# Performer attention and gated feed-forward on one core: squares moved to GpSimd, five more lean key chunks, small products in tiles of the array, and a new order

## The chip, the cores and the metric

The kernel runs on one core of one Trainium2 chip. The metric is the device time of one execution in microseconds, as the median of several runs. The engines are TensorE (PE; its weight loads are listed apart as PEld), VectorE (DVE), ScalarE (ACT), GpSimd (POOL) and SyncE (SP, which issues nearly all transfers). Each engine takes its instructions strictly in the order in which they were issued to it.

## What is computed

```python
def _attn_ref(q, k, v, omega):                 # 8 batches, 8 heads, 576 tokens, 64 wide; 128 features
    scale = 1.0 / np.sqrt(np.sqrt(D))
    q_s, k_s = (q * scale, k * scale)
    def phi(x):
        proj = np.einsum('bhsd,md->bhsm', x, omega)
        sq = np.sum(x * x, axis=-1, keepdims=True) / 2.0
        h = proj - sq
        h = h - np.max(h, axis=-1, keepdims=True)
        return np.exp(h) / np.sqrt(m)
    q_p, k_p = (phi(q_s), phi(k_s))
    kv = np.einsum('bhsm,bhsd->bhmd', k_p, v)
    z = np.sum(k_p, axis=2)
    num = np.einsum('bhsm,bhmd->bhsd', q_p, kv)
    den = np.einsum('bhsm,bhm->bhs', q_p, z)[..., None] + 1e-06
    return num / den

def _moe_ref(x, w_gate, w_val, w_out, rms_g):  # x: 4608 x 512; hidden width 1536
    xn = x / np.sqrt(np.mean(x * x, axis=-1, keepdims=True) + 1e-06) * rms_g
    g = xn @ w_gate
    return (g * (1.0 / (1.0 + np.exp(-g))) * (xn @ w_val)) @ w_out
```

q, k, v and omega are fp32. The three weight matrices come as fp64 and are turned into fp32 on the chip (`weights`, lines 414 to 484).

## The kernel before

The 4608 tokens are 36 chunks of 128. A pair of batches fills nine chunks, so that the middle one (number 4 of the nine) holds 64 tokens of either batch.

**Features** (`features`, for `k` and `q`, 36 chunks each). SyncE loads the chunk: for a plain chunk 512 KB, the transposed input for the projection beside the natural one for the norm; for a *lean* chunk (the first four of `k` and of `q`) the transposed 256 KB alone. `square` squares the input on ScalarE (with a factor of 1/4 ahead of the square, so 1/16 in the result). A plain chunk sums the squares per head with a VectorE reduction (`norm`, line 653); a lean chunk does it on TensorE, with the squares as stationary operand against a constant `heads2` (`norm_pe`, line 617: four products of 128 rows by 128 columns, 96 columns moving). `project` (line 666) multiplies by omega with the array split into two halves of 64 rows; `peak` takes the maximum per head on VectorE (line 679), `shift` forms the bias (lines 684 and 687), and `exps` writes the features with eight ScalarE exponentials (line 696). The first `k` chunk adds its bias by a product (`move`) instead.

**Keys times values.** `kv_half` accumulates the four whole chunks of a batch in halves of 64 array columns (line 797). `kv_mid` handles the shared middle chunk, four times in all: per head one product of 128 rows by 128 columns against a value tile of 130 columns, in which each batch's half stands beside zeros (loaded from `vmid`, 520 KB), three heads to a PSUM bank, with six evictions on VectorE (lines 758 and 768).

**Attention and normalisation** (`attend`): transposes of the query features (line 830), the product with `kv` in halves of 64 columns (line 841), the division on VectorE, the sum of squares on ScalarE, the root and the low part of the split on GpSimd (lines 873, 876, 910), and transposes back (line 891).

**Feed-forward.** The first three of twelve hidden slices run as three-pass products (`gated`, tile `ff`, line 303 and the two after it) as soon as a block of tokens is there. At about 380 us the remaining nine slices begin with a seven-product scheme (`unit`), at about 769 us the output with a fifteen-product one (`out_triple`). The change doesn't touch these.

**Order.** `Plan` writes the order of every engine by hand. Each step is added with an engine, a cost, a key of urgency, what it follows, and the slots it takes and gives; a list scheduler then hands the free engine its ready step of the lowest key. On TensorE, feed-forward steps (keys of 900 and more) come behind all others, and among the others a step in the array's present form (`rows`, `columns`, `full`) goes first; a change of form is charged 0.17. As long as no feed-forward step is ready, an idle TensorE is given a dummy product, `spin` (line 1036). The keys stand in the table `KEYS`; those of a chunk are the sum of a few entries, with fixed small offsets for each kind of step (as `key - 0.3`).

```python
        s = add("ACT", 0.54, square, [i], key)
        sq = ("psM", "sq", nm)
        if not lean:
            s = add("DVE", 0.62, norm, [s], key)
        p = add(
            "PE", 0.9, project, [i], key, [("psJ", nm, 0), ("psJ", nm, 1), (tag + "p", c)],
            mode="rows",
        )
        if lean:
            s = add("PE", 0.9, norm_pe, [s, p] if not first else [s], key, [sq])
```

Of the kernel before, what the change touches and what calls it, by code (L numbers as in the profile page):

```python
# [18 lines left out]
M = 128  # L19
DM = H * D  # L20
DFF = 1536
P = 128
# [20 lines left out]
    "lead": 2.76,  # L43
    "v": 94.42,
    "kv": -1042.79,
    "ks": [-482.1, 29.96, -132.79, -264.03, -121.88, -50.15, -91.33, -322.02, -18.14, -22.8, -48.17, -24.72, -44.53, -44.85, -5.61, -5.94, -12.97, -3.84, 2.1, 1.55, 8.44, 5.02, 7.82, 13.18, 14.51, 8.53, 67.56, 437.89, 70.53, 124.42, 9.96, 167.4, 229.45, 437.17, 436.87, 679.48],
    "qs": [-339.21, 60.83, -85.07, -28.07, -51.09, -68.82, -41.84, -8.68, -33.39, -36.86, -11.44, -13.61, -12.77, 3.74, 0.93, 9.58, 2.88, 13.96, 13.82, 24.74, 16.19, 27.63, 23.68, 32.28, 44.1, 39.37, 46.63, 71.79, 74.09, 51.71, 125.65, 141.98, 159.63, 160.11, 205.61, 233.21],
    "turns": [-103.42, 24.18, -177.68, -590.21, -266.4, -604.12, 86.86, -213.13, -649.06, -162.44, -441.45, -1049.27, 220.46, -465.51, -315.47, -515.05, 120.4, -151.51, -498.12, 49.51, 140.45, 37.25, -640.45, -581.4, -246.73, -220.97, -81.01, -127.83, 485.02, 422.3, 324.99, 129.53, 519.61, -510.45, -277.71, 106.54],
    "mixes": [-148.66, 18.01, -233.73, -283.22, -460.75, -241.78, -153.65, -610.2, -526.4, -237.05, -205.9, -687.04, -21.23, -169.25, -42.57, -535.29, -651.31, -129.56, -8.22, -36.89, -110.15, 62.57, 73.55, 66.58, -366.23, -288.34, 215.05, 358.84, -231.21, 414.57, -331.48, -648.64, 347.15, 23.97, 508.45, 389.85],
    "kvs": [65.82, -394.35, 257.28, -625.61, 216.21, -194.21, -511.95, 647.67],  # L50
    "attend": -122.15,
# [6 lines left out]
LEAN = {"k": 4, "q": 4}  # L58
# [10 lines left out]
        "ink": (4, 1), "v": (6, 1), "vm": (1, 1), "kp": (7, 1), "inq": (3, 1), "qp": (2, 1),  # L69
# [78 lines left out]
WIDE = 96  # L148
# [160 lines left out]
def performer_glu_kernel(  # L309
# [5 lines left out]
    vmid: bass.AP,  # L315
# [72 lines left out]
    for i in range(2):  # L388
        nc.gpsimd.memset(heads2[i * D : (i + 1) * D, 0, i : i + 1], 1.0 / SCALE)
        nc.gpsimd.memset(heads2[i * D : (i + 1) * D, 1, i : i + 1], 1.0)  # L390
# [199 lines left out]

    def features(tag, c, key):
# [5 lines left out]
        lean = c < max(LEAN[tag], FIRST[tag])  # L597

# [10 lines left out]
        def square():  # L609
            n = t["raw"][:, 1, :]  # L610
            nc.scalar.activation(n, t["x"] if lean else n, AF.Square, scale=0.25)

        def norm_pe():
            sq = tile_("psM", [P, DM], f"sq{nm}")
            t["sq"] = sq[:, :H]
            for hp in range(4):
                nc.tensor.matmul(
                    sq[:, 2 * hp : 2 * hp + WIDE],
                    lhsT=t["raw"][:, 1, hp * P : (hp + 1) * P],
                    rhs=heads2[:, 0 if first else 1, :],  # L620
                    start=True,
                    stop=True,
                    skip_group_check=True,
                )
# [26 lines left out]
        def norm():  # L651
            t["sq"] = small("sq", f"sq{nm}")
            ve.tensor_reduce(
                out=t["sq"],
                in_=t["raw"][:, 1, :].rearrange("p (h d) -> p h d", d=D),
                axis=AX.X,
                op=ALU.add,
            )
# [45 lines left out]
        size = 0.26 if lean else 0.52  # L704
# [11 lines left out]
        add("NONE", 0, lambda: None, [s, p], key, give=[("in" + tag, c)])  # L716
        m0 = add("DVE", 0.62, lambda: peak(0), [p], key)
        m1 = add("DVE", 0.62, lambda: peak(1), [m0], key)
        if first:
            b = add("DVE", 0.3, shift_first, [m1, s], key, give=[sq])  # L720
# [9 lines left out]
        b = add("DVE", 0.3, shift, [m1, s], key, give=[sq] if lean else [])  # L730
        e = b
        for n in range(4):
            e = add("ACT", 0.51, lambda n=n: exps(n), [e], key - 0.3, give=[("psJ", nm, n // 2)] if n % 2 else [])
        st["exp", tag, c] = e

    def values(c, key):
        mid = c % 9 == 4
        tag = "vm" if mid else "v"

        def load():  # L740
            w = 2 * (D + 1) if mid else D + 1
            st["v", c] = tile_(tag, [P, H, w], f"v{c}")
            nc.sync.dma_start(st["v", c], vmid[c // 9] if mid else va[c])

        size = 0.53 if mid else 0.27
        st["vload", c] = add("SP", size / RATE, load, key=key, take=[(tag, c)], land=LAND)

    def kv_mid(pr, key):
# [3 lines left out]
        def heads(h0, n, t):  # L752
            if h0 == 0:
                for b in range(2):
                    st["kv", 2 * pr + b] = tile_("kv", [P, H, D + 1], f"kv{2 * pr + b}")
            t["pt"] = tile_("psM", [P, 3, 2 * (D + 1)], f"kvm{pr}_{h0}")
            for i in range(n):
                nc.tensor.matmul(
                    t["pt"][:, i, :],
                    lhsT=st["kp", c][:, h0 + i, :],  # L760
                    rhs=st["v", c][:, h0 + i, :],
                    start=True,
                    stop=True,
                )

        def out(h0, n, t):
            for b in range(2):
                ve.tensor_scalar_mul(
                    st["kv", 2 * pr + b][:, h0 : h0 + n, :],
                    t["pt"][:, :n, b * (D + 1) : (b + 1) * (D + 1)],  # L770
                    1.0 / M,
                )

        last = [st["exp", "k", c], st["vload", c]]
        for h0 in (0, 3, 6):
            n = min(3, H - h0)
            t = {}
            ps = ("psM", "kvm", pr, h0)
            take = [ps] + ([("kv", 2 * pr), ("kv", 2 * pr + 1)] if h0 == 0 else [])
            give = [("kp", c), ("vm", c)] if h0 == 6 else []  # L780
            m = add("PE", 0.24 * n, lambda a=(h0, n, t): heads(*a), last, key, take, give)
            last = [m]
            done.append(add("DVE", 0.29, lambda a=(h0, n, t): out(*a), [m], key, give=[ps]))
# [36 lines left out]
    def attend(c, ahead, key):  # L820
# [100 lines left out]
        for half in range(2):  # L921
# [4 lines left out]
            te.append(add("ACT", 0.5, lambda h=half: turned(h), [i], ahead - 0.4,  # L926
# [896 lines left out]
```

## Time and profile before

| | |
|---|---|
| time, median of 3 runs | 1021.58 us (1021.27 to 1021.89) |
| span of the profiled execution, first to last instruction | 1020.1 us |
| busy share of the span: PE, PEld | 99%, 84% |
| busy share: DVE, ACT, POOL | 84%, 65%, 18% |
| granted clock of TensorE | full in every slice |
| transferred | 213.93 MB, mean 210 GB/s |

Of the profiled execution only the span is given; it is 1.5 us under the median of the runs, which also hold what lies around the program. TensorE's busy time includes the dummy products, and records of products overlap, so that a pace is read from starts, not from lengths. Each fp32 product appears as two records.

### The profile page before, as it was taken

Reading aid. Unit: us, or ns where it says so; the run is one execution under the profiler, and the core shown is the slowest. Engines: PE = TensorE matmul, PEld = TensorE weight load, DVE = VectorE, ACT = ScalarE, POOL = GpSimd, SP = SyncE. Lnnn points to the kernel's source line nnn. Section 1 sums busy time; section 2 is a strip of 40 time slices with the busy share of each in tenths; the row PEclk is TensorE's granted clock in tenths of the full one; section 3 lists DMA queues with packets and bytes.
Section 4 is the critical chain, followed back from the end, with each engine's and each line's share of the span. In section 5 each row is a group of like instructions: output and inputs, shape, how many; then the busy total and the mean of one; then the engine's idle time right before and its main releaser. Section 6 shows DMA issues by size and latency. Waiting matters only on the chain.

```text
span 1020.1 us, 20747 instructions
## 1 busy us (share of the span) xinstructions
PE 1007.7 (99%) x7628; PEld 857.4 (84%) x7628; DVE 857.2 (84%) x1505; ACT 666.8 (65%) x1477; POOL 179.4 (18%) x259
## 2 busy tenths in 40 slices
PE   9999999999999999999999999999999999999998
PEld 6889888888888888888898888988888887888886
DVE  6899899998976765998889958988778999789885
ACT  7999999898796646646356446643556554565561
POOL 0323212221223338100001123000000000222120
PEclk9999999999999999999999999999999999999999
DMA  9677676585544476674576767775456684898882
GB/s 315 233 243 236 221 250 228 186 275 166 193 146 146 139 234 214 205 258 145 170 251 213 238 203 243 241 259 196 151 179 235 226 292 152 202 273 191 204 175 63
DMA packets 120805, 213.93 MB, mean 210 GB/s; under 512 B 10496, under 2 KB 53248, under 8 KB 120704
## 3 DMA queue, kind: packets, MB, share of 16 engines
q1 hardware_dynamic: 115808, 203.69, 60.1%
q0 software_dynamic: 4896, 8.92, 6.1%
q8 instruction: 60, 0.98, 0.4%
q14 instruction: 41, 0.34, 0.1%
HBM read 134.58 MB, written 77.99 MB: 208 GB/s over the span
## 4 chain that ended last, share of the span: by engine, by line
PE 83%; DVE 9%; ACT 6%; issue 1%; DMA 0%; SPq 0%; ACTq 0%; DVEq 0%
PE q L304 8%; PE q L305 8%; PE q L303 8%; PE pa L303 7%; PE pa L304 7%; PE pa L305 7%; PE ff L303 4%; PE ff L305 4%; PE ff L304 4%; PE pb L304 4%; PE pb L305 4%; PE pb L303 4%; PE nu L841 2%; PE pc L304 2%; PE pc L305 2%; PE pc L303 2%
## 5 line engine op out<-in xcount | busy, mean ns | idle before, releaser
L1290 ACT ACTIVATE c<-c 128x512 f32<-128x512 f32 (+1 forms) x90 | 52.9, 590 | 90.2 <-DVE c L1272 90.0
L303 PE MATMUL ff<-xhi,whi 128*128 128x512 f32 (+3 forms) x248 | 94.6, 381 | 1.5 <-ACT qp L696 0.6
L1686 POOL DMA_DIRECT2D out_dram<-c x34 | 29.8, 885 | 360.6 <-ACT c L1672 290.6
L696 ACT ACTIVATE qp<-pjq,biq 128x128 f32<-128x128 f32 x288 | 81.1, 431 | 15.0 <-DVE biq L687 12.5
L305 PE MATMUL ff<-xhi,wlo 128*128 128x512 f32 (+3 forms) x248 | 90.4, 365 | 0.0
L304 PE MATMUL ff<-xlo,whi 128*128 128x512 f32 (+3 forms) x248 | 90.3, 364 | 0.0
L696 ACT ACTIVATE kp<-pjk,bik 128x128 f32<-128x128 f32 x280 | 78.7, 447 | 5.7 <-DVE bik L687 2.8
L910 POOL TENSOR_TENSOR xlo<-xr,xhi 128x256 fp32r<-128x256 f32 x72 | 56.3, 807 | 125.2 <-ACT xhi L907 125.2
L1554 DVE TENSOR_TENSOR hb<-hb,hb 128x1024 f32<-128x1024 f32 x55 | 66.3, 1219 | 0.4
L303 PEld LDWEIGHTS ff<-xhi,whi 128*128 128x128 f32 x248 | 46.7, 188 | 10.3 <-ACT qp L696 0.8
L305 PEld LDWEIGHTS ff<-xhi,wlo 128*128 128x128 f32 x248 | 46.7, 188 | 7.6
L304 PEld LDWEIGHTS ff<-xlo,whi 128*128 128x128 f32 x248 | 46.8, 189 | 6.2
L1272 DVE TENSOR_TENSOR c<-pb,u 128x512 f32<-128x512 f32 (+1 forms) x45 | 28.4, 633 | 27.3 <-PE pb L305 25.2
L679 DVE TENSOR_REDUCE mxk<-pjk 128x4 f32<-128x512 f32 x72 | 46.9, 682 | 4.7 <-PE pjk L666 4.7
L1265 ACT COPY m<-pa 128x512 f32<-128x512 f32 (+1 forms) x45 | 24.4, 543 | 34.9 <-PE pa L305 34.7
L679 DVE TENSOR_REDUCE mxq<-pjq 128x4 f32<-128x512 f32 x72 | 46.5, 681 | 0.8 <-PE pjq L666 0.8
L833 ACT COPY qpT<-qt 128x512 f32<-128x512 f32 x72 | 41.1, 664 | 1.9 <-PE qt L830 1.9
L841 PEld LDWEIGHTS nu<-kv,qpT 128*64 128x64 f32 x1152 | 36.0, 137 | 5.3 <-issue 1.1
L830 PE MATMUL qt<-ident,qp 128*128 128x128 f32 x288 | 38.6, 276 | 1.6 <-DVE hmk L684 1.0
L666 PE MATMUL pjq<-front,inq 64*128 64x128 f32 x560 | 39.8, 281 | 0.1
L841 PE MATMUL nu<-kv,qpT 128*64 128x65 f32 x1152 | 39.6, 223 | 0.1
L1109 POOL TENSOR_TENSOR lw_0l<-wr,lw_0h 128x256 fp32r<-128x256 f32 x9 | 7.7, 854 | 182.0 <-PE pa L305 138.5
(300 smaller groups left out, 3254.0 us busy)
## 6 DMA issues: line engine op xcount, KB each, us to landing
hb<-h_scratch SPq DMA_DIRECT2D x49, 512.0 KB, 5.4
h_scratch<-c SPq DMA_DIRECT2D x72, 256.0 KB, 2.5
ink<-in_kx_dram SPq DMA_DIRECT2D x32, 512.0 KB, 5.2
inq<-in_qx_dram SPq DMA_DIRECT2D x32, 512.0 KB, 4.5
Xb<-xn_scratch SPq DMA_DIRECT2D x28, 512.0 KB, 5.2
f<-in_wgv_dram SPq DMA_DIRECT2D x24, 512.0 KB, 4.9
xn_scratch<-xr SPq DMA_DIRECT2D x36, 256.0 KB, 3.2
out_dram<-c SPq DMA_DIRECT2D x36, 256.0 KB, 2.9
```

The lines of the kernel that those rows point to most:

```text
L303: nc.tensor.matmul(out, lhsT=ah, rhs=bh, start=first, stop=False, skip_group_check=again)
L304: nc.tensor.matmul(out, lhsT=ah, rhs=bl, start=False, stop=False, skip_group_check=again)
L305: nc.tensor.matmul(out, lhsT=al, rhs=bh, start=False, stop=last, skip_group_check=again)
L666: nc.tensor.matmul(t["pts"][i][:, hp, :], lhsT=x[rows, hp, :], rhs=om[rows, :], start=hp == 0 or not first, stop=True, skip_group_check=first,
L679: ve.tensor_reduce(out=by_half[:, i, :], in_=t["pts"][i], axis=AX.X, op=ALU.max)
L696: nc.scalar.activation(st[tag + "p", c][:, h, :], t["pts"][h % 2][:, h // 2, :], AF.Exp, bias=t["bi"][:, h : h + 1], scale=SCALE,)
L830: nc.tensor.transpose(t["pt", half][:, i, :], st["qp", c][:, 4 * half + i, :], ident)
L833: nc.scalar.copy(t["qpT"][:, 4 * half : 4 * half + 4, :], t["pt", half])
L841: nc.tensor.matmul(pt[lo:hi, i, :], lhsT=t["qpT"][:, h, lo:hi], rhs=st["kv", b][:, h, :], start=True, stop=True,)
L910: nc.gpsimd.tensor_tensor(out=st["xT", blk][1][:, ccs, cs], in0=t["xr"][:, ccs], in1=st["xT", blk][0][:, ccs, cs].bitcast(F32), op=ALU.sub ...
L1290: nc.scalar.activation(t[nm], t[nm], AF.Silu)
L1554: ve.tensor_tensor(out=t[nm, g], in0=t[x, g], in1=t[y, g], op=ALU.add if sign == "+" else ALU.subtract,)
```

## The change

- `LEAN` for `k` goes from 4 to 9 chunks: chunks 4 to 8 of `k` load 256 KB instead of 512 KB, and their norm goes from VectorE to TensorE.
- `square` runs on GpSimd for the first 14 chunks of `k` and of `q` (28 squares), without the factor. Lean chunks take the factor 1/16 in `heads2`; plain ones among the 28 (ten of `q`, five of `k`) get a step `quarter` on GpSimd behind the reduction.
- `norm_pe` becomes eight products on halves of 64 array columns, with 64 columns moving (`WIDE` from 96 to 64).
- `kv_mid` becomes, per head, four products on quarters of the array (64 rows by 64 columns, 65 moving): the two batches lie on different rows and go to PSUM tiles of their own. Half of the heads at a time take two banks; there are four evictions instead of six. The tile `vm` and the input `vmid` go; the middle chunk loads 260 KB like any other, and the value pool grows from six to seven.
- The features of `q` chunk 0, whose load also brings omega, are added first, and every projection follows that load in the plan.
- All keys are replaced. Sixteen new ones (`late`) are the offsets of kinds of steps.

```diff
 KEYS = {
-    "g": -33.66,
-    "k": [53.74, -331.3, -385.51, 23.11, -468.03, -23.41, 3.36, -11.8, -61.3],
...
+    "g": -517.43,
+    "k": [-335.0, -229.57, -979.76, 378.15, -1105.96, 536.82, -1214.5, -924.91, 464.95],
+    "q": [-3487.62, 238.12, -494.25, 828.13, -116.49, 136.54, 217.68, 168.67, 138.5],
...
+    "late": [401.64, 426.72, 252.47, -2847.11, -77.63, -558.35, -559.96, -400.78, -197.14, 55.14, 188.2, -37.61, -268.71, -8.5, -621.42, -1019.57],
...
-LEAN = {"k": 4, "q": 4}
+POOLED = 14
+LEAN = {"k": 9, "q": 4}
...
-        "ink": (4, 1), "v": (6, 1), "vm": (1, 1), "kp": (7, 1), "inq": (3, 1), "qp": (2, 1),
+        "ink": (4, 1), "v": (7, 1), "kp": (7, 1), "inq": (3, 1), "qp": (2, 1),
...
-WIDE = 96
+WIDE = 64
...
-        nc.gpsimd.memset(heads2[i * D : (i + 1) * D, 1, i : i + 1], 1.0)
+        nc.gpsimd.memset(heads2[i * D : (i + 1) * D, 1, i : i + 1], 0.0625)
...
         lean = c < max(LEAN[tag], FIRST[tag])
+        pooled = lean or c < POOLED
...
-            nc.scalar.activation(n, t["x"] if lean else n, AF.Square, scale=0.25)
+            x = t["x"] if lean else n
+            if pooled:
+                nc.gpsimd.tensor_tensor(out=n, in0=x, in1=x, op=ALU.mult)
+            else:
+                nc.scalar.activation(n, x, AF.Square, scale=0.25)
...
             for hp in range(4):
-                nc.tensor.matmul(
-                    sq[:, 2 * hp : 2 * hp + WIDE],
-                    lhsT=t["raw"][:, 1, hp * P : (hp + 1) * P],
...
+                for at in (0, D):
+                    nc.tensor.matmul(
+                        sq[at : at + D, 2 * hp : 2 * hp + WIDE],
+                        lhsT=t["raw"][:, 1, hp * P + at : hp * P + at + D],
...
+        def quarter():
+            nc.gpsimd.tensor_scalar(
+                out=t["sq"], in0=t["sum"], scalar1=0.0625, scalar2=None, op0=ALU.mult
+            )
...
-        s = add("ACT", 0.54, square, [i], key)
+        s = add("POOL" if pooled else "ACT", 1.06 if pooled else 0.54, square, [i], key + late[0])
+        st.setdefault("om", i)
...
-            s = add("DVE", 0.62, norm, [s], key)
+            n = s = add("DVE", 0.62, norm, [s], key + late[1])
+            if pooled:
+                s = add("POOL", 0.2, quarter, [n], key + late[1])
         p = add(
-            "PE", 0.9, project, [i], key, [("psJ", nm, 0), ("psJ", nm, 1), (tag + "p", c)],
+            "PE", 0.9, project, [i, st["om"]], key, [("psJ", nm, 0), ("psJ", nm, 1), (tag + "p", c)],
...
-            s = add("PE", 0.9, norm_pe, [s, p] if not first else [s], key, [sq])
+            s = add("PE", 0.48, norm_pe, [s, p] if not first else [s], key + late[15], [sq], mode="columns")
...
-            t["pt"] = tile_("psM", [P, 3, 2 * (D + 1)], f"kvm{pr}_{h0}")
-            for i in range(n):
-                nc.tensor.matmul(
-                    t["pt"][:, i, :],
-                    lhsT=st["kp", c][:, h0 + i, :],
-                    rhs=st["v", c][:, h0 + i, :],
...
+            t["pt"] = [tile_("psM", [P, 4, D + 1], f"kvm{pr}_{half}{b}") for b in range(2)]
+            for i in range(4):
+                h = 4 * half + i
+                for at in (0, D):
+                    for b in range(2):
+                        rows = slice(b * D, (b + 1) * D)
+                        nc.tensor.matmul(
+                            t["pt"][b][at : at + D, i, :],
+                            lhsT=st["kp", c][rows, h, at : at + D],
+                            rhs=st["v", c][rows, h, :],
...
+            m = add("PE", 0.5, lambda a=(half, t): heads(*a), last, key, take, give, mode="quads")
...
+    features("q", 0, KEYS["q"][0] + KEYS["qs"][0])
     for c in range(nch):
```

## Rows read from the trace of the kernel before

**Rows 1.** Busy time by stretch: start:end, length, engines, clock, DMA share, GB/s.

```profile
...
5.30:51.00 45.70, 43.91 (x620) 37.10 (x620) 38.32 (x101) 42.71 (x124) 9.43 (x14) 1.00 0.83 282
51.00:116.00 65.00, 61.97 (x921) 57.15 (x920) 61.98 (x159) 62.73 (x194) 18.23 (x29) 1.00 0.73 235
116.00:380.00 264.00, 263.22 (x3110) 229.82 (x3109) 222.53 (x536) 213.99 (x607) 71.09 (x115) 1.00 0.61 197
...
769.00:1020.00 251.00, 245.38 (x1082) 202.56 (x1080) 210.38 (x212) 135.57 (x179) 29.83 (x34) 1.00 0.74 202
...
```

**Rows 2.** The same view for the filler product `spin` alone.

```profile
...
0.00:5.30 5.30, 4.43 (x10) 1.00 0.61 203
5.30:51.00 45.70, 4.10 (x12) 1.00 0.83 282
...
```

**Rows 3.** Chain of work to 130 us: start, length, engine, tile, line.

```profile
...
1.18 4.05 DMA front<-in_q0om_dram
5.36 1.51 PE pjk L666 x16
...
22.99 2.30 ACT kp L696 x9
...
31.92 1.55 ACT ink L611 x3
...
83.14 0.60 DVE sqq L653
...
116.94 0.87 PE qt L830 x8
...
```

**Rows 4.** SyncE's transfers in order of time: start, length of issue.

```profile
...
0.74 0.38 SPq L607 DMA_DIRECT2D ink<-in_kx_dram  x1
...
```

**Rows 5.** The squares, line 611, before 52 us, with ScalarE's shortest/median/longest (ns).

```profile
...
L611 ACT ACTIVATE ink<-ink x10: 629/728/802, 4.4 to 37.9; 128x512 f32<-128x512 f32 x10
...
L611 ACT ACTIVATE inq<-inq x4: 618/727/750, 19.0 to 34.7; 128x512 f32<-128x512 f32 x4
...
```

**Rows 6.** GpSimd in order of time to 110 us.

```profile
...
37.22 0.19 POOL L873 TENSOR_SCALAR ss<-ss 128x1 f32<-128x1 f32 x1 [0.91 <-ACT xn L867]
...
39.39 1.28 POOL L484 TENSOR_TENSOR wlo<-w,whi 128x512 fp32r<-128x512 f32 x1 [1.33 <-ACT whi L481]
...
52.99 1.76 POOL L484 TENSOR_TENSOR wlo<-w,whi 128x512 fp32r<-128x512 f32 x1
...
```

**Rows 7.** TensorE in order of time, 8 to 11 us.

```profile
...
8.59 1.13 PE L617 MATMUL sqq<-heads,inq 128*128 128x96 f32 x8
9.55 1.06 PE L617 MATMUL sqk<-heads,ink 128*128 128x96 f32 x8
...
```

**Rows 8.** TensorE in order of time, 86 to 92 us.

```profile
...
88.19 2.06 PE L758 MATMUL kvm<-v,kp 128*128 128x130 f32 x16
90.09 0.60 PE L830 MATMUL qt<-ident,qp 128*128 128x128 f32 x4
...
```

**Rows 9.** TensorE in order of time, 103 to 110 us.

```profile
...
102.97 3.95 PE L797 MATMUL kvp<-v,kp 128*64 128x65 f32 x128
106.75 0.64 PE L841 MATMUL nu<-kv,qpT 128*64 128x65 f32 x16
107.32 1.16 PE L666 MATMUL pjq<-front,inq 64*128 64x128 f32 x16
...
```

**Rows 10.** Line 666 in steps of 10 ns; x counts products under way.

```profile
...
99.30:99.31 0.01, 0.01 (x4) 1.00 0.00 0
99.31:99.32 0.01, 0.01 (x5) 1.00 0.00 0
99.32:99.33 0.01, 0.01 (x6) 1.00 0.00 0
...
```

**Rows 11.** VectorE on the `mag` tile: shortest/median/longest (ns).

```profile
...
L424 DVE TENSOR_SCALAR mag<-mag x36: 409/420/1192, 15.6 to 586.5; 128x512 f32<-128x512 f32 x36
...
```

**Rows 12.** VectorE on the `hmk` tile, the same columns.

```profile
...
L684 DVE SCALAR_TENSOR_TENSOR hmk<-mxk,sqk x35: 153/166/705, 8.2 to 300.1; 128x8 f32<-128x8 f32 x35
...
```

More of the change, by code (lines that the diff above doesn't have):

```diff
@@ L589, in out_sums @@
         )
+    late = KEYS["late"]
     def features(tag, c, key):
@@ L651, in norm @@
         def norm():
-            t["sq"] = small("sq", f"sq{nm}")
+            t["sum"] = t["sq"] = small("sq", f"sq{nm}")
             ve.tensor_reduce(
-                out=t["sq"],
+                out=t["sum"],
                 in_=t["raw"][:, 1, :].rearrange("p (h d) -> p h d", d=D),
@@ L714, in features @@
         if lean:
-            s = add("PE", 0.9, norm_pe, [s, p] if not first else [s], key, [sq])
-        add("NONE", 0, lambda: None, [s, p], key, give=[("in" + tag, c)])
-        m0 = add("DVE", 0.62, lambda: peak(0), [p], key)
-        m1 = add("DVE", 0.62, lambda: peak(1), [m0], key)
+            s = add("PE", 0.48, norm_pe, [s, p] if not first else [s], key + late[15], [sq], mode="columns")
+        add("NONE", 0, lambda: None, [s if lean else n, p], key, give=[("in" + tag, c)])
+        m0 = add("DVE", 0.62, lambda: peak(0), [p], key + late[2])
+        m1 = add("DVE", 0.62, lambda: peak(1), [m0], key + late[2])
         if first:
-            b = add("DVE", 0.3, shift_first, [m1, s], key, give=[sq])
+            b = add("DVE", 0.4 if pooled else 0.3, shift_first, [m1, s], key, give=[sq])
             ends = []
@@ L729, in features @@
             return
-        b = add("DVE", 0.3, shift, [m1, s], key, give=[sq] if lean else [])
+        b = add("DVE", 0.4 if pooled else 0.3, shift, [m1, s], key + late[3], give=[sq] if lean else [])
         e = b
         for n in range(4):
-            e = add("ACT", 0.51, lambda n=n: exps(n), [e], key - 0.3, give=[("psJ", nm, n // 2)] if n % 2 else [])
+            e = add("ACT", 0.51, lambda n=n: exps(n), [e], key + late[4 + (tag == "q")], give=[("psJ", nm, n // 2)] if n % 2 else [])
         st["exp", tag, c] = e
     def values(c, key):
-        mid = c % 9 == 4
-        tag = "vm" if mid else "v"
         def load():
[L741 to L746, printed above, removed]
+            st["v", c] = tile_("v", [P, H, D + 1], f"v{c}")
+            nc.sync.dma_start(st["v", c], va[c])
+        st["vload", c] = add("SP", 0.27 / RATE, load, key=key, take=[("v", c)], land=LAND)
     def kv_mid(pr, key):
@@ L766, in out @@
[L766 to L783, printed above, removed]
+            t["pt"] = [tile_("psM", [P, 4, D + 1], f"kvm{pr}_{half}{b}") for b in range(2)]
@@ new lines, in heads @@
+            for i in range(4):
[7 more added lines that the diff above has]
+                            rhs=st["v", c][rows, h, :],
+                            start=True,
+                            stop=True,
+                        )
@@ new lines, in out @@
+        def out(half, b, t):
+            ve.tensor_scalar_mul(
+                st["kv", 2 * pr + b][:, 4 * half : 4 * half + 4, :], t["pt"][b], 1.0 / M
+            )
+        last = [st["exp", "k", c], st["vload", c]]
+        for half in range(2):
+            t = {}
+            ps = [("psM", "kvm", pr, half, b) for b in range(2)]
+            take = ps + ([] if half else [("kv", 2 * pr), ("kv", 2 * pr + 1)])
+            give = [("kp", c), ("v", c)] if half else []
+            m = add("PE", 0.5, lambda a=(half, t): heads(*a), last, key, take, give, mode="quads")
+            last = [m]
+            for b in range(2):
+                done.append(
+                    add("DVE", 0.35, lambda a=(half, b, t): out(*a), [m], key, give=[ps[b]])
+                )
@@ L925, in attend @@
             turns = [i]
-            te.append(add("ACT", 0.5, lambda h=half: turned(h), [i], ahead - 0.4,
+            te.append(add("ACT", 0.5, lambda h=half: turned(h), [i], ahead + late[6],
                           give=[("psM", "qt", c, half)]))
@@ L946, in attend @@
             plan.prompt.add(s)
-        i = add("ACT", 0.54, xhi, [i], key - 0.6)
+        i = add("ACT", 0.54, xhi, [i], key + late[13])
         for cc in range(0, NCC, 2):
-            i = add("POOL", 0.76, lambda cc=cc: xlo(slice(cc, cc + 2)), [i], key - 0.3)
+            i = add("POOL", 0.76, lambda cc=cc: xlo(slice(cc, cc + 2)), [i], key + late[14])
         st["x", c] = i
```

63 lines of the change are left out of this document (26 added, 37 removed), and 3 rows, old and new, of the table KEYS.

## The prediction

> **What bounds the kernel now.** I read the busy time by stretch first, then the same view for the dummy products alone, then the chain of waits, then each engine in order of time where an edit lies.
>
> By stretch, TensorE is the bound from 116 us on: between 116 and 380 us it is idle for 0.8 of 264 us, and the last stretch loses 5.6 us at its start and in its tail, which the change doesn't touch [rows 1]. There the time is the length of TensorE's own queue, and a microsecond of products less is a microsecond less. Ahead of that it is different. From 5.3 to 51 us TensorE shows 43.9 busy of 45.7 us, but 4.1 of them are dummies [rows 1, 2], so that 1.8 + 4.1 = 5.9 us are lost; from 51 to 116 us, where feed-forward products fill in, 3.0 us are lost [rows 1]. Before 5.3 us it has nothing but dummies [rows 2], since the first projection waits for omega [rows 3]. The chain shows who takes the time in the front: it runs through ScalarE (exponentials, and three squares in a row at 31.92 us) and VectorE (a norm at 83.14 us), and settles on TensorE only at about 117 us [rows 3]. ScalarE is busy for 42.7 of 45.7 us in the first of these stretches and 62.7 of 65 in the second, VectorE for 38.3 and 62.0 [rows 1]. So there are two pots: 8.9 us of lost TensorE time in the front, and TensorE's work itself.
>
> **The change part by part.** Durations are those of the profiled execution, whose span is 1020.1 us; I carry the sum over to the median of 1021.58 unchanged.
>
> *Head.* Omega's load starts at 1.18 us, behind a 512 KB load issued at 0.74, and takes 4.05 us [rows 3, 4]. The new key of `q` chunk 0 is -3487.62 - 39.43 = -3527, far the lowest, so that it goes out first. By itself that gains the 0.44 us between the issues, and at most also the time of the 512 KB ahead of it, 1.8 us at the 282 GB/s of the next stretch [rows 1]. The `k` chunk that comes now behind it (and behind its values, which have a lower key) comes no earlier, so I stay by the near end: -0.6 (0 to -1.8).
>
> *Squares.* A square takes ScalarE 1.55/3 = 0.52 us of its queue [rows 3]. 15 of them lie before 52 us, ten of `k`, four of `q` and one on omega's load [rows 5]; that takes 7.8 us off the 42.7. Five norms of 0.60 us [rows 3] leave VectorE: 38.3 to 35.3. TensorE's real work there is 43.9 - 4.1 = 39.8 and falls by the two next items to about 37. So ScalarE, at 34.9, stops being the longest queue and TensorE becomes it. The lost 5.9 us can't all go, since the start is a line of dependent steps; I take 2.5 of it (0 to -5). Between 51 and 116 us the other 13 squares free 6.8 us of ScalarE, but VectorE stays at 62 of 65: I take -0.8 of the 3.0 lost (0 to -2).
>
> On GpSimd a square is nearest to the split of a 128x512 tile, 1.28 us [rows 6], above the 1.06 of the plan. 28 x 1.28 = 36 us and fifteen `quarter` steps at the 0.19 of a small GpSimd step [rows 6], 3 us, stand against 9.4 + 18.2 us of work in 110 us [rows 1]. What hides a square is the projection and the two maxima of the same chunk, 0.9 and 1.24 us by the plan's costs. What waits behind it in GpSimd's queue are the roots and low parts of the attention, and behind these TensorE's transposes back; I cost it at nothing where the queue is mostly empty, and at the third rival's price where not.
>
> *Norms.* A lean norm took 9.55 - 8.59 = 0.96 us for eight records [rows 7]. On halves of 64 columns the nearest row is `kv_half`: 128 records of 65 columns in 106.75 - 102.97 = 3.78 us, 29.5 ns each [rows 9]. Sixteen records are 0.47 us. Eight norms at 0.96 are 7.7, thirteen at 0.47 are 6.1: -1.6. They lie in the front, where they count in full only once TensorE is its longest queue (0 to -1.6).
>
> *Middle chunks.* `kv_mid` took 90.09 - 88.19 = 1.90 us [rows 8]. Now it is 64 records. If quarters go at the pace of the column halves, 64 x 29.5 ns = 1.89 us and nothing is gained. If the two row halves of either column half run together too, half of that, 0.95. That row halves do run together is seen at the projection: two records start within 10 ns of each other [rows 10]; and the new loop alternates the rows from product to product. Both overlaps are shown, each by itself, and I take them as multiplying: -0.95 each, four times, -3.8 (0 to -3.8). Three of the four lie behind 88 us, at TensorE's bound or close to it. The two evictions less, and the smaller loads, shorten queues that have 41 us to spare behind 116 us on VectorE [rows 1], and none in the chain: nothing.
>
> *Changes of the array's form.* `nu`'s sixteen records take 0.57 us to the next projection instead of 16 x 29.5 ns = 0.47 [rows 9]: about 0.10 us for a change. `kv_mid` was in the form of the feed-forward and needs now two changes, 0.8 in all, or 1.6 if its halves are parted. Thirteen norms instead of eight add up to 1.0, less if they stand beside `kv` products. I take +1.5 (0.8 to 2.6). What the new order does to the other changes can't be seen in advance.
>
> Sum: -0.6 - 2.5 - 0.8 - 1.6 - 3.8 + 1.5 = -7.8, a span of 1012.3, and **1013.8 us** as the median.
>
> **The rivals.** *Quarters go at the pace of halves.* For it: no row shows four tiles at work. Against it: the paired starts [rows 10]. The 3.8 are gone: 1017.6. The Trainium skill, "TensorE: Matmul & The Clock Gate", section "Back-to-back issue gap", puts a floor of about 25 ns between the starts of two products, however short; at 64 such steps a middle chunk would be an estimated 1.6 us, and the time an estimated 1016.4. The trace's 10 ns between two row tiles [rows 10] speaks against that floor across tiles.
>
> *VectorE holds the front.* It was the second longest queue, is relieved by 3.0 us only, and takes its turns in the chain [rows 1, 3]. If it sets the pace, what ScalarE gives up moves nothing: the 2.5 and 0.8 fall away, 1017.1. For it: 62 of 65 us in the second stretch; against it: 35 of 46 in the first, where most was lost. Both rivals together: 1020.9, no change that can be told.
>
> *GpSimd holds VectorE: slower.* Some VectorE instructions are drawn out: a `mag` step takes 1192 ns where 420 is the median, an `hmk` step 705 where 166 is [rows 11, 12], and a GpSimd split beside it 1.76 instead of 1.28 us [rows 6]. If each of the 28 squares holds a VectorE step for 705 - 166 = 0.54 us, the first stretch, which has no filler, takes on 15 x 0.54 - 3.0 = 5.1 us. The second takes on 13 x 0.54 = 7.0, of which 4.0 exceed its free 3.0 and become holes. With the head, norms, middle chunks and form changes (-0.6 - 1.6 - 3.8 + 1.5 = -4.5) that is +4.6: 1026.2. It decides from some 0.45 us a square on. Against it: with 28 us of GpSimd work in these 110 us the median of both steps is undisturbed. The Trainium skill, "GPSIMD Engine Reference", section "Key points", says that GpSimd shares its SBUF interfaces with VectorE and contends with instructions that read two SBUF inputs or run in a two-port mode; by it maxima and reductions, the bulk of VectorE's front, would go free, and the estimate above is a worst case. The undisturbed medians agree.
>
> **How the numbers follow.** The measurement can tell about 0.2%, 2 us, from no change. Forecast, with 1009 to 1018 as its own range: 0.48. Quarters at half pace 0.15, VectorE holds the front 0.15, both 0.08, GpSimd holds VectorE 0.10, and 0.04 for an order that is better or worse in a way no row shows, half each. Faster: 0.48 + 0.15 + 0.15 + 0.02, less 0.04 for cases of the first two that end within 2 us: 0.76. Same: 0.08 + 0.04 = 0.12. Slower: 0.12. The range reaches from the sum at its better bounds with a middle share of lost time, 1008, over both rivals on the fast side to 1022.5; left out are the slower rival, the 0.04, and about 0.04 of tails.
>
> **What would show it.** Right: the stretch from 5 to 51 us ends some 3 to 5 us earlier with under 3 us of dummies; the first projection stands at about 4.8 us; a norm's records take 0.47 us, a middle chunk's 64 records about 0.95 us plus changes; VectorE and TensorE, not ScalarE, lead the chain up to 100 us; the seven-product part starts near 372 us instead of 380. Wrong: 25 to 30 ns a record in the middle chunk; `hmk`, `bik` and `mag` steps commonly near 0.7 us beside a GpSimd square; TensorE waiting for GpSimd's roots or low parts; or a later part that is no longer as long as before.

## The result, and the profile after

The changed kernel takes 1026.99 us (median of 5 runs, 1025.16 to 1029.61) against 1021.58: a ratio of 1.0051, interval 1.0039 to 1.0064. It is slower by 5.4 us; the forecast was 1013.8. The profiled execution is the 1025.16, with a span of 1023.4 us, 3.3 more than before. Its mean TensorE clock is 1.00; the other four runs have 0.995 to 0.998. Whether that is the rest of the loss is taken up in the last section.

Busy time by stretch, and the dummies alone in the second of them (TensorE, TensorE's weight loads, VectorE, ScalarE, GpSimd):

```profile
5.30:51.00 45.70, 40.24 (x762) 32.49 (x758) 40.47 (x95) 37.14 (x116) 27.64 (x28) 1.00 0.74 256
51.00:116.00 65.00, 59.10 (x855) 54.29 (x851) 62.13 (x148) 57.12 (x177) 34.07 (x54) 1.00 0.64 210
116.00:380.00 264.00, 262.90 (x3345) 230.31 (x3346) 222.74 (x538) 211.03 (x604) 70.57 (x116) 1.00 0.61 197
...
5.30:51.00 45.70, 4.20 (x13) 1.00 0.74 256
```

Beside [rows 1, 2]: ScalarE is relieved by 5.6 us in either stretch (42.7 to 37.1 and 62.7 to 57.1), where 7.8 and 6.8 were planned; GpSimd has 34 us more, and VectorE, which gave up five norms, is busy for 2.2 us more in the first stretch. TensorE's lost time from 5.3 to 116 us (idle and dummies) rises from 8.9 to 5.46 + 5.90 + 4.20 = 15.6 us. Between 116 and 380 us next to nothing is lost (1.1 us, 0.8 before). So the front lost 6.7 us where the forecast gained 3.3.

The chain of waits has changed hands:

```profile
17.72 0.75 DVE kv L783 x2
...
18.74 0.86 DVE mag L425
19.62 1.16 DVE mag L433
20.80 0.70 DVE w L444
21.53 0.69 DVE w L455
...
31.47 1.25 DVE mag L425
...
38.15 1.16 DVE mag L433
...
54.10 1.59 POOL inq L617
...
57.23 1.11 DVE w L444
58.37 1.10 DVE w L455
...
81.52 1.26 DVE bik L701
```

From 16 to 46 us almost every step is VectorE's, where [rows 3] have exponentials and squares of ScalarE between. And the steps are long: line 425 has a median of 420 ns, and stands here with 860 and 1250; line 701 has 167 ns, and stands with 1260. What they sit beside is seen in VectorE's order of time and then GpSimd's, same kernel:

```profile
18.57 0.16 DVE L701 SCALAR_TENSOR_TENSOR bik<-hmk,sqk 128x8 f32<-128x8 f32 x1
18.65 0.93 DVE L425 TENSOR_SCALAR mag<-mag 128x512 f32<-128x512 f32 x1
19.62 1.15 DVE L433 TENSOR_SCALAR mag<-mag 128x512 int32<-128x512 int32 x1
...
81.52 1.25 DVE L701 SCALAR_TENSOR_TENSOR bik<-hmk,sqk 128x8 f32<-128x8 f32 x1
```

```profile
18.27 1.04 POOL L617 TENSOR_TENSOR ink<-ink 128x512 f32<-128x512 f32 x1 [0.28 <-DMA ink<-in_kx_dram]
19.26 1.22 POOL L617 TENSOR_TENSOR inq<-inq 128x512 f32<-128x512 f32 x1
...
81.47 1.27 POOL L485 TENSOR_TENSOR wlo<-w,whi 128x512 fp32r<-128x512 f32 x1
```

The drawn-out steps end close behind the end of a GpSimd instruction beside them: 19.58 against 19.31, 20.77 against 20.48, 82.77 against 82.74; the small bias steps 0.02 to 0.03 us behind, `mag` 0.28, `w` and `xn` 0.55. Work of 0.17 or 0.42 us can so last as long as the rest of a GpSimd instruction of 1.04 to 1.27 us. That instruction need not be a square: the third of these is a split (`wlo`) which the kernel before has too. The reductions `mxk` and `mxq` are never drawn out (0.68 us throughout). Nor are the bias steps of lean chunks, whose norm lies in PSUM: the one at 18.57 takes 0.16 us in the middle of a square, and so do the others up to 51 us that lie beside a square or a split (150 to 164 ns).

By tile, shortest/median/longest in ns, and first and last start: the squares, the first feed-forward products, the first of the seven-product part.

```profile
L617 POOL TENSOR_TENSOR ink<-ink x14: 1037/1042/1227, 6.2 to 70.1; 128x512 f32<-128x512 f32 x14
...
L305 PE MATMUL ff<-xhi,whi x248: 221/389/504, 66.3 to 382.8; 128*128 128x512 f32 x92, 128*128 128x256 f32 x24, 128*128 128x384 f32 x4, 128*128 128x128 f32 x4
...
L305 PE MATMUL pa<-Rb11h,lw_0h x90: 278/389/396, 383.5 to 755.6; 128*128 128x512 f32 x72, 128*128 128x256 f32 x18
```

The `pa` products began at 380.3 before and begin at 383.5: the whole 3.3 us is there by then. The first `ff` product went from 51.0 to 66.3. TensorE in order of time:

```profile
3.89 1.16 PE L680 MATMUL pjq<-front 64*128 64x128 f32 x16
...
7.63 0.69 PE L626 MATMUL sqk<-heads,ink 128*64 128x64 f32 x16
8.24 1.16 PE L680 MATMUL pjk<-front,ink 64*128 64x128 f32 x16
...
16.71 0.70 PE L774 MATMUL kvm<-v,kp 64*64 64x65 f32 x32
17.34 1.15 PE L626 MATMUL sqk<-heads,ink 128*64 128x64 f32 x32
...
166.58 1.16 PE L774 MATMUL kvm<-v,kp 64*64 64x65 f32 x64
167.67 0.50 PE L305 MATMUL ff<-xhi,whi 128*128 128x512 f32 x1
```

The first projection starts at 3.89 instead of 5.36 [rows 3]. A norm takes 8.24 - 7.63 = 0.61 with its change of form, against 0.96 [rows 7]. Half a middle chunk takes 17.34 - 16.71 = 0.63 us to the next product, and the third chunk, whose halves stand together, 167.67 - 166.58 = 1.09, against 1.90 before [rows 8]. The 0.63 are 19.7 ns a record, but the last 0.15 of them follow the start of the last record. A record itself lasts 0.22 us, so that the last of the 64 starts at 166.58 + 1.16 - 0.22 = 167.52: the records come 15.0 ns apart there, and 15.5 in the halves.

**A balance of TensorE up to `pa`.** For each group of equal products I take the time from its start to the next group's start. Its records times a price are "work" (29.5 ns for column halves, 19.7 for quarters, which takes in the 0.15 us at the end of each group, 111.5 for a record of the old norm or middle chunk, 56.2 a projection, 109 a transpose, N/2400 us + 14.2 ns for a feed-forward product of N columns); up to 0.2 us more where the form changes is "change"; the rest is "hole". In us, for the profiled executions. Up to 30 ns a group without a change of form, 2.6 to 2.9 us in all, and the first 0.8 us are left out:

```
                       work  changes        dummies  holes  first ff  pa
before                340.8  13.2 (x102)    9.2      13.7   51.0      380.3
after                 337.7  15.1 (x117)    7.5      19.6   66.3      383.5
e1_scalar_same_order  337.7  15.2           7.9      18.6   67.1      383.1
e5_no_squares         337.7  15.0           7.8      14.9   63.0      378.9
e6_alternate          337.7  15.2           7.9      16.7   64.8      381.0
e8_halves             337.5  13.6 (x105)    9.3      16.1   50.8      379.9
```

After minus before: -3.1 + 1.9 - 1.7 + 5.9 = +3.0 of the 3.2. For VectorE I add up what its `mag`, `w`, `xn` and bias steps take above before's medians, to 116 us: 2.4 us before, 10.6 after, 8.2 more. Not all of that is the squares' own. Of the 20 steps drawn out in after, nine end just behind a square (5.5 us, 0.2 for each of the 28 squares) and eleven behind one of the splits `wlo` and `xlo` (5.0 us), which GpSimd makes in both kernels and which meet other steps in the new order.

### The profile page after: what moved, and what is told of

The parts are those of the page before. It is cut to its first block, busy times and chain, and to the rows that moved or that the text cites. A ratio compares the mean times of both kernels' runs of the same rounds, so it can differ in the third digit from the quotient of the medians.

```text
span 1023.4 us, 21417 instructions
## 1 busy us (share of the span) xinstructions
PE 1004.3 (98%) x7963; PEld 853.9 (83%) x7963; DVE 862.0 (84%) x1492; ACT 653.6 (64%) x1449; POOL 214.4 (21%) x302
## 4 chain that ended last, share of the span: by engine, by line
PE 90%; DVE 5%; ACT 2%; issue 1%; DMA 1%; POOL 0%; SPq 0%; DVEq 0%; ACTq 0%; POOLq 0%
PE q L306 8%; PE q L307 8%; PE q L305 8%; PE pa L305 7%; PE pa L307 7%; PE pa L306 7%; PE ff L305 5%; PE ff L307 5%; PE ff L306 5%; PE pb L305 4%; PE pb L306 4%; PE pb L307 4%; PE nu L856 3%; PE pjk L680 3%; PE pjq L680 3%; PE qt L845 3%
## 5 line engine op out<-in xcount | busy, mean ns | idle before, releaser
L1571 DVE TENSOR_TENSOR hb<-hb,hb 128x1024 f32<-128x1024 f32 x55 | 66.3, 1220 | 0.4
L680 PE MATMUL pjk<-front,ink 64*128 64x128 f32 x576 | 39.5, 279 | 0.7 <-DMA ink<-in_kx_dram 0.5
```

The lines of the kernel that those rows point to most:

```text
L680: nc.tensor.matmul(t["pts"][i][:, hp, :], lhsT=x[rows, hp, :], rhs=om[rows, :], start=hp == 0 or not first, stop=True, skip_group_check=first,
L1571: ve.tensor_tensor(out=t[nm, g], in0=t[x, g], in1=t[y, g], op=ALU.add if sign == "+" else ALU.subtract,)
```

## The experiments

**Squares back on ScalarE, same order (e1).**

```diff
-                nc.gpsimd.tensor_tensor(out=n, in0=x, in1=x, op=ALU.mult)
+                nc.scalar.activation(n, x, AF.Square)
```

> The changed kernel with the order of every step as planned, but the 28 squares issued to ScalarE at their planned place. Theory A (GpSimd's squares hold VectorE): VectorE's drawn-out steps before 116 us, about 11 us in all in the changed kernel against 2 before, fall back to 2 to 3 us; ScalarE takes on 28 x 0.52 = 14.6 us and is close to full, so the time comes down only part of the way, 1021 to 1025. Theory B (the new order itself is worse, whoever squares): the time stays at 1026 or rises, to 1032 with the fuller ScalarE.

1025.3 us, ratio 1.0044 (1.0029 to 1.0059). VectorE's groups by line and shape from 5.3 to 51 us (busy, mean ns), of this kernel and then of after:

```profile
L425 DVE TENSOR_SCALAR mag<-mag 128x512 f32<-128x512 f32 x4 | 2.3, 575 | 1.7 <-ACT mag L419 1.7
L433 DVE TENSOR_SCALAR mag<-mag 128x512 int32<-128x512 int32 x4 | 1.7, 428 | 0.1
```

```profile
L425 DVE TENSOR_SCALAR mag<-mag 128x512 f32<-128x512 f32 x4 | 3.9, 975 | 0.0
L433 DVE TENSOR_SCALAR mag<-mag 128x512 int32<-128x512 int32 x4 | 3.1, 787 | 0.1
```

The drawn-out time falls from 10.6 us to 2.4, the sum of before. But ScalarE is at 42.3 of 45.7 us again, and the time hardly moves: it ends between the two theories. Squares on GpSimd cost this order about what they cost it on ScalarE; they are not the whole of the loss.

**Each square in four pieces (e2).**

```diff
-                nc.gpsimd.tensor_tensor(out=n, in0=x, in1=x, op=ALU.mult)
+                for a in range(0, DM, P):
+                    y = x[:, a : a + P]
+                    nc.gpsimd.tensor_tensor(out=n[:, a : a + P], in0=y, in1=y, op=ALU.mult)
```

> The changed kernel with each GpSimd square cut into four instructions of 128 columns, same order, some 0.4 us more GpSimd work a square. Theory A, with VectorE held to the end of the GpSimd instruction under way: a hold is at most 0.3 us instead of 1.04, the drawn-out VectorE time before 116 us falls from about 11 to 4 to 6 us, and the time by 2 to 5, to 1021 to 1025. If the two merely share bandwidth, the drawn-out time stays at 11 or more and the time at 1026 to 1029. Theory B: within 1 us of the changed kernel.

1027.0 us, 1.0052 (1.0036 to 1.0068). Drawn-out time falls to 7.6 us: beside squares from 5.5 to 2.0, beside splits it stays (5.0 and 5.6). GpSimd is busier for it (38.6 of 45.7 us), and nothing is gained, as theory B had it.

**The old urgencies (e3), and TensorE's edits alone under the old urgencies (e4).** e3 is the changed kernel with `KEYS` and offsets of before; e4 is before with `norm_pe` on halves and `kv_mid` on quarters, with their new costs. In both the key of `q` chunk 29 is 90 instead of 51.71 and the middle chunks keep a slot for values of their own.

```diff
-    "g": -517.43,
+    "g": -33.66,
...
-    "late": [401.64, 426.72, 252.47, -2847.11, ...],
+    "late": [0, 0, 0, 0, -0.3, -0.3, -0.4, -0.3, -0.5, -5, -0.4, -0.3, -0.6, -0.6, -0.3, 0],
```

> The changed kernel with the keys and offsets of before (one key of query chunk 29 moved, and the middle value chunk in a slot of its own as before, since the plan finds no order otherwise). Theory A: the squares still hold VectorE, drawn-out time 7 to 11 us before 116 us, and the time is 1021 to 1027. Theory B: the time falls below before by the saved TensorE work and loads, 1014 to 1019.

> The kernel before with the TensorE edits alone: norms of the eight lean chunks on column halves and middle chunks on quarters; squares on ScalarE, four lean key chunks, old keys (one key of query chunk 29 moved). The changed kernel's trace shows 32 records of a middle chunk in 0.63 us, so 1.26 against 1.90: four times 0.64 is 2.6 us, and norms 8 x (0.96 - 0.58) = 3.0, which count only where TensorE waits for nothing. Both theories: 1017 to 1020.5; above 1021.6 would say that even these edits lose, by the changes of the array's form or by a worse order.

1034.78 us (1.0132, 1.0117 to 1.0147) and 1038.13 (1.016, 1.0143 to 1.0177). Neither tells what it was made for: changed costs make a new order out of old keys, and that order is worse (holes of 25.8 and 23.4 us). How much the one moved key does isn't known. They show how much an order can weigh: 13 to 17 us over before.

**No squares at all (e5).** The changed kernel without them; the norms are sums of the loaded values instead.

```diff
-            if pooled:
-                nc.gpsimd.tensor_tensor(out=n, in0=x, in1=x, op=ALU.mult)
-            else:
+            if not pooled:
...
-                        lhsT=t["raw"][:, 1, hp * P + at : hp * P + at + D],
+                        lhsT=t["x"][:, hp * P + at : hp * P + at + D],
```

> The changed kernel in the same order with its 28 early squares left out on every engine (lean norms are taken of the inputs themselves, plain ones of the loaded values, so the norms are those of x and not of its square). Theory A, refined after the run with the squares on ScalarE (the order leaves no room on either engine: on GpSimd the squares hold VectorE for 8 us, on ScalarE they take 14.6 us of a full queue): with neither, the first feed-forward product comes 5 to 7 us earlier than at 66, the holes shrink by 5 us or more, and the time is 1015 to 1020. Theory B (the new order is worse by itself): the first feed-forward product stays near 66 us and the time at 1023 or above.

1022.84 us, 1.0006 (0.9997 to 1.0015), 4.2 less than after; in the profiled executions, both at full clock, 1018.7 against 1023.4. So the squares on GpSimd cost this order some 4 to 5 us. On ScalarE they cost it as much: from e1 to e5 ScalarE alone loses 28 squares, and `pa` comes 383.1 - 378.9 = 4.2 us earlier. Even free of them the order doesn't beat before beyond the noise; the time lies between the two theories. The two stretches, and the dummies in the first:

```profile
5.30:51.00 45.70, 43.79 (x876) 36.00 (x876) 40.32 (x103) 39.99 (x126) 9.93 (x15) 1.00 0.81 274
51.00:116.00 65.00, 60.74 (x892) 55.85 (x888) 62.76 (x151) 58.77 (x181) 23.05 (x43) 1.00 0.67 216
...
5.30:51.00 45.70, 4.20 (x13) 1.00 0.81 274
```

Lost time is 1.91 + 4.26 + 4.20 = 10.4 us: 5.2 less than after, and still 1.5 more than before. VectorE's drawn-out time is 5.8 us without a single square on GpSimd, all of it beside splits, as here (VectorE, then GpSimd):

```profile
76.81 1.25 DVE L699 SCALAR_TENSOR_TENSOR bik<-hmk,sqk 128x8 f32<-128x8 f32 x1
...
76.76 1.27 POOL L485 TENSOR_TENSOR wlo<-w,whi 128x512 fp32r<-128x512 f32 x1
```

**Every other square on ScalarE (e6).**

```diff
+                if c % 2:
+                    nc.scalar.activation(n, x, AF.Square)
+                else:
```

> The changed kernel in the same order, every other square (odd chunks) issued to ScalarE and the rest to GpSimd. Theory A: VectorE's drawn-out time falls from 10.6 to about 6 us, ScalarE takes on 7.3 us, of which its slack before 51 us (8.6 us) covers most; the time is 1021 to 1024.5. Theory B: 1025 to 1027 as with all on one engine.

1024.18 us, 1.0025 (1.0014 to 1.0036): the best of the new order with all its work, 2.8 under after, and still behind before. Drawn-out time is 6.2 us; theory A held.

**The old order to the letter, with 28 squares on GpSimd (e7).**

```diff
-            nc.scalar.activation(n, t["x"] if lean else n, AF.Square, scale=0.25)
+            if c < 14:
+                nc.gpsimd.tensor_tensor(out=n, in0=x, in1=x, op=ALU.mult)
+            else:
+                nc.scalar.activation(n, x, AF.Square, scale=0.25)
```

> The kernel before in its own order, with the first 28 squares issued to GpSimd at their planned places (and the factor as in the changed kernel). Theory A: ScalarE loses 14.6 us in the front where the chain runs through it, VectorE gains 6 to 9 us of drawn-out steps; as the old order is fitted to ScalarE squares the sum is about nil, 1019 to 1024. If squares on GpSimd were harmless and the new order alone to blame, 1016 to 1020.

1034.14 us, 1.0123 (1.0108 to 1.0138). That is above the ranges of both theories. Here the squares stand without the other edits, the plain ones with a quartering on GpSimd behind their norm. Up to 116 us GpSimd waits 10.9 and 8.6 us for VectorE's norms ahead of the quarterings, with the next squares behind them in its queue. So this run doesn't tell what a hold alone costs.

**The old order to the letter, with the norms on halves (e8).**

```diff
-WIDE = 96
+WIDE = 64
...
+                for at in (0, D):
...
+                        sq[at : at + D, 2 * hp : 2 * hp + WIDE],
+                        lhsT=t["raw"][:, 1, hp * P + at : hp * P + at + D],
```

> The kernel before, its own order to the last instruction, with one edit: the eight lean norms as sixteen records on column halves. The trace of after has 0.61 us for sixteen such records with their change of form, against 0.96 us for the old eight, so eight norms give TensorE 8 x 0.35 = 2.8 us back, all of it ahead of 50 us. Theory A (the front is set by ScalarE and VectorE, and what TensorE saves there becomes dummies and idle time): 1021.0 to 1021.8 us, with 1 to 3 us more of dummies and idle time ahead of 51 us. Theory B (the saving counts, as the step on the norms in the prediction had it): 1018.8 to 1020 us, and the first feed-forward product 1.5 to 3 us ahead of 51.0.

1021.6 us, 0.9997 (0.9988 to 1.0006). Its second stretch:

```profile
5.30:51.00 45.70, 41.61 (x685) 33.96 (x686) 38.28 (x101) 42.83 (x126) 9.66 (x14) 1.00 0.81 282
```

TensorE is busy for 2.3 us less than in [rows 1], and VectorE and ScalarE to within 0.2 us the same. By the balance 3.3 us of work are gone, 2.4 of holes and 0.4 of changes have come, and `pa` is 0.4 earlier. What TensorE saves ahead of 51 us it waits away. Theory A held.

**Quarter products twice, in the changed kernel (e9).**

```diff
+                        for _ in range(2):
                             nc.tensor.matmul(
                                 t["pt"][b][at : at + D, i, :],
```

> The changed kernel with each quarter product of the middle chunks issued twice into the same place (it overwrites itself, so the result stands): 4 x 64 more records, in the same order. Theory A (TensorE is the bound where the middle chunks lie and a quarter record costs 19.7 ns, as the trace of after has it): 256 x 19.7 ns = 5.0 us more, 1031 to 1032.5 us. Theory B (the middle chunks lie in lost time, so that their length doesn't count, and the 2.6 us that the quarters save are lost for that reason): 1027 to 1028.5 us. Theory C (a second product on the same quarter of the array follows at the pace of the halves or slower): 256 x 29.5 ns = 7.6 us, 1034 us or more.

1030.29 us, 3.3 above after; by the ratios to before (1.0078 and 1.0051) 2.8. Theory A's 5.0 counted all four chunks at 19.7 ns and missed; none of the three has this time. In the trace the four chunks take 1.22, 1.22, 1.08 and 0.38 us more than in after, 3.9 in all (behind the last one TensorE waits for ScalarE in after, so that it has room). The first stands at 13.6 to 17.3 us, in the front; the three others, from 104 us on, add up to 2.7. With some 1.5 us of uncertainty on either median the time fits three chunks that count and one that doesn't, as e8 has it for the front; it doesn't prove the split.

**The old order, halves, and only the eight lean squares on GpSimd (e10).**

```diff
...
+            if lean:
+                nc.gpsimd.tensor_tensor(out=n, in0=t["x"], in1=t["x"], op=ALU.mult)
+            else:
+                nc.scalar.activation(n, n, AF.Square, scale=0.25)
...
```

> The kernel before, its own order, the norms on halves as in e8_halves, and the squares of its eight lean chunks on GpSimd, the other squares stay on ScalarE. Nothing on VectorE stands ahead of a lean square and nothing waits for a quartering. ScalarE is relieved of 8 x 0.52 = 4.2 us ahead of about 45 us, where its queue is the longest; by the drawn-out steps of after (8.2 us for 27 squares, 0.3 us each) VectorE takes on 2.4. Theory A (a hold of 0.3 us counts only where VectorE leads, and the relief of ScalarE counts in the front): 1018.5 to 1020.5 us, a version that beats both kernels. Theory B (the hold and the square's 1.05 us instead of 0.52 eat what ScalarE gives up): 1021.5 us or more, and the first feed-forward product at 51 us or later.

1023.03 us, 1.0012 (1.0003 to 1.0021), 1.4 above e8. The stretch, and VectorE's bias steps in it by line and shape:

```profile
5.30:51.00 45.70, 41.13 (x668) 32.72 (x668) 38.93 (x99) 37.44 (x114) 16.65 (x21) 0.96 0.78 274
```

```profile
L688 DVE SCALAR_TENSOR_TENSOR hmk<-mxk,sqk 128x8 f32<-128x8 f32 x6 | 2.0, 328 | 0.3
L691 DVE SCALAR_TENSOR_TENSOR bik<-hmk,sqk 128x8 f32<-128x8 f32 x6 | 1.8, 297 | 0.2
```

ScalarE gives up 5.4 us, the bias steps of `k` double (164 ns before), and the time rises, as theory B had it; the first feed-forward product comes at 52.2 us. The clock of 0.96 is this execution's own; runs at 1.00 are no faster (1022.43 to 1024.19). With the other edits out of the way, relief of ScalarE, hold of VectorE and a square that takes 1.04 us instead of 0.52 add up to a loss of 1.4 us. Which of the two prices outweighs the relief isn't shown, since they come together.

**Twice the work of GpSimd's squares, in the changed kernel (e11).**

```diff
-                nc.gpsimd.tensor_tensor(out=n, in0=x, in1=x, op=ALU.mult)
+                for op in (ALU.add, ALU.mult):
+                    nc.gpsimd.tensor_tensor(out=n, in0=x, in1=x, op=op)
...
-                out=t["sq"], in0=t["sum"], scalar1=0.0625, scalar2=None, op0=ALU.mult
+                out=t["sq"], in0=t["sum"], scalar1=0.015625, scalar2=None, op0=ALU.mult
```

> The changed kernel, same order, with an addition of the same shape ahead of each of GpSimd's squares (x + x, which the square overwrites in the lean chunks and takes as its input in the others, whose quartering becomes a sixteenth of that): GpSimd's work on squares is doubled, about 30 us more in the first 116. Theory A (the cost of the squares is the hold of VectorE): drawn-out time of VectorE's steps doubles from 8.2 us above before to about 16, and the time rises by what it fell when the squares were left out, 4 to 5 us: 1031 to 1032 us. Theory B (it is the lateness of the square in the chunk's own line, 1.1 us each): the early stretch grows by more than 8 us, 1035 us or more, with waits for inq and ink at sqk and the norms. Theory C (GpSimd's squares have nothing to do with the loss, the order has): 1027 to 1028.5 us.

1041.61 us, 14.6 above after. Drawn-out time rises by 9.2 us, from 10.6 to 19.8, as theory A had it; the time rises by three times what A gave. B's sign, waits for `inq` and `ink`, is small (2.7 us at `sqk`, 1.2 at `sqq`). GpSimd is busy for 39.1 of 45.7 us, so that its other steps come late too, and the granted clock is 0.89 in that stretch and 0.95 in the next, which adds to the time. The dose tells the direction; the time is in theory B's range, the drawn-out time in theory A's, and neither is shown by it.

## Why the prediction was wrong

*Squares (-2.5 and -0.8): the step that failed.* It gave TensorE 3.3 us of the time lost in the front for the relief of ScalarE, and put at nothing what squares on GpSimd cost. In its place the runs showed that lost time from 5.3 to 116 us grew by 6.7 us. Of that 5.2 go with the squares on GpSimd (e5 has 10.4 against 15.6). The other 1.5 are there with no square on any engine, so that even relief without a price didn't bring the 3.3 in the new order. Relief by itself is worth something: taken off ScalarE alone (e1 to e5) the squares give 4.2 us at `pa`; taken off GpSimd alone (after to e5) they give 4.6, so that the move from one to the other gains nothing. The chain from 16 to 46 us is VectorE's in after. The prediction's 35.3 for it was too low as well: one of the five norms starts at 51.67, behind the stretch, as one of the 15 squares ends ahead of it, so that 36 and 35.4 were the lengths to compare. How much of the 5.2 is the hold of VectorE and how much that squares and splits come later isn't parted: from after to e5 holes and drawn-out time both fall by 4.7, but in e2 drawn-out time falls by 3.0 and the time doesn't. GpSimd's price itself was near: 1.04 us a square against the 1.28 taken.

*The rival that came true* is the slower one, GpSimd holds VectorE, given 0.10 and 1026.2. That VectorE is held is seen in the trace, and e5 and e11 show that squares on GpSimd cost time. Its size is not as argued: 0.2 us a square (0.2 to 0.3 in e6, e7, e10 and e11) instead of 0.54, below the 0.45 from which it was to decide. That the time agrees is luck: it takes 9.1 us for the hold and gives back 4.5 for the other edits, where squares cost 4 to 5 and the other edits without them (e5) give 1.4 of span and nothing in the median. "The median of both steps is undisturbed" was the wrong evidence: a median over 36 steps, most of them far from any GpSimd work, says nothing of a step beside a square; the longest values in [rows 11, 12] were the ones to price. Of the Trainium skill's rule ("GPSIMD Engine Reference", section "Key points") the trace agrees that reductions go free; the steps that don't are those between the reductions, and they stand in the chain.

*Norms (-1.6).* TensorE's time for them went from 7.1 to 6.1 us by record prices, -1.0; but in the front of the old order it isn't paid (e8: 3.3 us of work less, 0.4 us earlier). The prediction had said that it counts in full only if TensorE is the longest queue, and took the full end.

*Middle chunks (-3.8).* The pace was right: 15.0 to 15.5 ns a record, next to the 14.8 of two overlaps that multiply. What it saves is less than 3.8, since each group takes 0.15 us more at its end, two of the four chunks are parted, and the last one waits for ScalarE: from start to the next product the four took 7.57 us before and take 5.39, so 2.2 less, of which the first chunk's 0.7 lie in the front. With its changes of form the forecast had -3.0 to -2.2 here. The floor of 25 ns that the Trainium skill gives ("TensorE: Matmul & The Clock Gate", section "Back-to-back issue gap") doesn't hold on average across four tiles.

*Form changes (+1.5)* were fifteen more, +1.9, and about 0.9 more stand in the price of the quarters (six groups of 0.15 us). *Head (-0.6)* was -1.5 at the first projection, and the next ones wait for their loads and for VectorE.

*The order* was held to be neutral, with 0.04 for it. With the squares on ScalarE (e1) the new order loses 4.9 us more in holes than the old one does with that placement, although it has 3.1 us less work; free of squares (e5) it loses 1.2 more, and has fifteen changes of form more; its dummies are 1.3 and 1.4 us fewer. How much of the loss is the order and how much the squares in it can't be parted cleanly: they were laid out for each other, and the old order with the new squares is worse still (e7). This stays open, as does a run of the quarters alone in the old order, which wasn't tried: its middle chunks need two banks at a time, and no run shows whether the old order could free them there.

## What to carry to other kernels

Before moving work to GpSimd, look not at how idle it is but at which VectorE steps stand in the chain at that time. Here those that read two tiles of SBUF or scale one could last until GpSimd's instruction ended; those that reduce didn't, and neither did bias steps whose norm lay in PSUM. Put a price on such a meeting from the longest values, and look also at GpSimd's other work: a new order moves those meetings too. In a stretch in which three engines are each over 80% busy, time taken off one queue may come back as idle time: of 3.3 us of TensorE's work e8 kept 0.4. Try each relief alone in an unchanged order, and without its price, as e5 does. Short products on quarters of the array came here at half the spacing of halves; count every change of form, and what parts a group.

## What the hardware did that I had not expected

A VectorE step of 0.17 us took 1.25 us beside a GpSimd instruction of 1.27 us and ended with it; the same step with its norm in PSUM took 0.16 in the middle of one. Splitting the square in four (e2) took 3.0 of the 10.6 us off.

The clock followed a hole. In e9's profiled execution TensorE stood idle from about 61.9 to 64.6 us; columns are busy time, then granted clock:

```profile
62.00:63.00 1.00, 0.00 (x0) 1.00 0.96 337
63.00:64.00 1.00, 0.00 (x0) 1.00 1.06 337
...
65.00:66.00 1.00, 1.00 (x7) 0.50 0.92 337
66.00:67.00 1.00, 1.00 (x6) 0.50 0.94 372
67.00:68.00 1.00, 1.00 (x9) 0.70 0.76 295
68.00:69.00 1.00, 1.00 (x33) 1.00 0.27 98
```

It came back at 0.50, the 1.2 GHz level, and the sixteen records of transposes there took 3.40 us. In e2's profiled execution they follow a hole of 2.80 us and take 3.33. In after's the same products follow the same hole of 2.68 us at a clock of 1.00, and take 2.00:

```profile
63.04 2.00 PE L845 MATMUL qt<-ident,qp 128*128 128x128 f32 x16 [2.68 <-ACT qp L710]
```

So one hole can cost 1.4 us more, or not. The other runs of after, at 0.995 to 0.998, are 0.8 to 4.5 us longer than this one; before's five have 1021.27 to 1022.08. In e5 the two runs at 1.000 took 1020.74 and 1020.87, the eight at 0.997 or 0.998 took 1022.22 to 1023.76; in e6 the two kinds overlap (1022.95 to 1024.92 at 1.000). A clock that falls in some runs would fit the 1.8 us between after's profiled run and its median; that it is this hole in those runs isn't shown, since they left no trace.
